# Clustered attention and two mixers on one core: the place of the scores in an attention step, of the first u tiles and of the second batch's u

## The chip, the cores and the metric

The kernel runs on one core of one Trainium2 chip. Its time is the device time of one execution in microseconds (us). The kernel before takes 904.54 us (median of 3 runs, 904.22 to 904.85). A core has five engines, each with an instruction queue of its own that it works through in order: TensorE (PE in the profile; its weight loads, PEld, overlap its matmuls), VectorE (DVE), ScalarE (ACT), GpSimd (POOL) and SyncE (SP), which here only issues transfers (DMA).

## The reference

Attention in which a query sees only the keys of its own cluster, then two mixer layers. All inputs are 32-bit or 64-bit floats on the host.

```python
# attention: batch 2, heads 8, sequence 768, head size 64, 16 clusters
q_assign = argmax(q_n . c_n); k_assign = argmax(k_n . c_n)
scores = where(q_assign == k_assign, q @ k.T / 8, -1e9)
x = softmax(scores) @ v                     # as [2, 768, 512]
# first mixer: U [768, 32], V [32, 768], 4*512 hidden channels
u = x + ((x.T @ U) @ V).T
x = u + relu(u @ w_ch1) @ w_ch2
# second mixer: 256 hidden tokens, 1536 hidden channels
u = x + (relu(x.T @ w_tok1) @ w_tok2).T
out = u + relu(u @ w_ch1) @ w_ch2
```

## The kernel before

**Precision.** Operands of the large products are split into two parts, hi and lo (`rnd` rounds to the hi part, mostly on ACT; `sub` makes the lo part, mostly on DVE), and a product is the sum of hi x hi, hi x lo and lo x hi. The mixers' weights come as 64-bit floats and are turned into 32-bit ones on the chip by `conv` (one operation on ACT, four on DVE for each block of 512 columns) and then split. One call of `tick` moves this conversion on by one block through its stages.

**Attention** works in head pairs: 2 batches x 4 pairs, 12 tiles of 128 queries each, 96 tiles. For tile n, `s_mm` makes the scores (four matmuls of 384 columns into banks 0 and 1 or 2 and 3 of PSUM, by turns), `s_max` takes the negated row maximum on DVE (`nm`), `s_exp` the exponential on ACT with its row sum (`p32`, three buffers), `t_mm` transposes the six blocks of 128 columns on PE into banks 4 and 5, four blocks to a bank, `t_out` makes the hi part (`pth`, ACT) and the lo part (`ptl`, DVE) of each finished bank, and `pv` multiplies with v. A group of three tiles is transposed while the group before is multiplied with v; `pv_out` and `merge` bring its result back to rows, and `merge_out` scales it into `xn`.

The order is written by hand in `step(n)`: the exponential of tile n+1, the transposes that fill a bank and their hi and lo parts, the scores and maximum of tile n+2, the other transposes, then work of other parts at set steps (`mid`, then PV, then `late`). A step with n even finishes one bank, one with n odd two. At set steps of a pair stand the cluster assignment of the next pair (`scores`, `argmax_a`, `argmax_b`), its copies into the stacks `qk` by some 22 transfers on SP, the load and split of v, the product of `xn` with U (`zmm`), and for the first batch the addition of (x.T U) V (`zadd`). Seven conversion ticks stand in the last 20 steps.

**The first mixer** works in three passes over 512 of the 1536 tokens (batch and sequence in one row of tokens), with 16 blocks of 128 hidden channels each. `half_slots` gives turns: `hidden(k+1)` with its relu and split (`hidden_out`: `gh` on ACT, `gl` on DVE), then `outmm(k)`, 12 matmuls of 512 columns each. In the first pass each half slot also takes one tick, so the weights are converted just ahead of their use; the split ones go through DRAM for the two later passes. `umm` transposes a tile of `xn` on PE and `umm_out` makes its hi and lo parts `uh` and `ul`, the mixer's input. Four tiles of u (0 to 3) are made between attention and the first hidden layer; the others, and the second batch's `zadd`, in `rest_of_u`, one operation in each half slot from the start of the first pass. Near the end of a pass `outmm` adds uh and ul into `x2` (`f == nf - 3`) and then the result to it; `x2` lies over `xn` with its rows in another order, c by batch and token, so that its first tokens lie over tiles of both batches.

**The second mixer** first mixes tokens (`tok(0)`, `tok(1)`), beside the third pass of the first mixer and the first pass of its own channel part, then has three passes of 12 blocks.

## Time and profile before

| what | value |
|---|---|
| time, median of 3 runs | 904.54 us |
| the profiled execution | 905.5 us |
| its span | 903.7 us |
| PE busy | 801.8 us (89%) |
| weight loads (PEld) busy | 654.9 us (72%) |
| DVE busy | 535.1 us (59%) |
| ACT busy | 352.9 us (39%) |
| POOL busy | 101.4 us (11%) |
| mean granted TensorE clock | 0.976 of full |

The profile is of one execution. Busy time is the sum of an engine's instructions; matmuls overlap, so a PE that is always busy is not yet PE at its peak. Attention takes the span up to about 360 us, the two mixers the rest. A timeline row gives the start, the length, the engine, the line of the kernel, and the operation with its output and inputs by their names in the kernel; in square brackets stands how long the engine had been idle before it, and what it waited for. An instruction's length reaches past the start of the next one on its engine, so what an operation costs its engine is read from start to start.

### The profile page before, as it was taken

What the parts mean: (1) busy time and instruction counts of PE and PEld (TensorE: products, weight loads), DVE (VectorE), ACT (ScalarE), POOL (GpSimd) and SP (SyncE); (2) the same over time, 40 slices, a digit from 0 to 9 for tenths busy, and PEclk for the clock granted to TensorE, in tenths of its full rate; (3) what the DMA queues carried; (4) which work ended last, traced back from release to release, by engine and by line L of the source; (5) the groups of instructions that cost most, each with busy time, mean ns of one, the idle gap of its engine ahead of it and who ended that gap; (6) DMA issues with size and microseconds to landing.
All of it is one profiled execution on the core that took longest, in us unless ns stands there. A gap on an engine that the chain in (4) does not pass through costs nothing.

```text
span 903.7 us, 11114 instructions
## 1 busy us (share of the span) xinstructions
PE 801.8 (89%) x3989; PEld 654.9 (72%) x3989; DVE 535.1 (59%) x857; ACT 352.9 (39%) x679; POOL 101.4 (11%) x88
## 2 busy tenths in 40 slices
PE   1787878888888877989988999999999999999998
PEld 0566666777666665866656888888888888888886
DVE  3778667676768577699889778766233123212213
ACT  1675656656656665344343323343122111111110
POOL 1110110110101001000002222322120011000000
PEclk9998999899999999899999999999999999999999
DMA  8725152433425313377888899997545444654762
GB/s 203 158 61 132 46 139 53 115 79 88 90 77 113 113 48 106 126 267 271 282 299 290 326 377 370 404 399 301 201 137 175 140 140 140 250 191 164 268 196 94
DMA packets 59238, 167.78 MB, mean 186 GB/s; under 512 B 8656, under 2 KB 16848, under 8 KB 59184
## 3 DMA queue, kind: packets, MB, share of 16 engines
q1 hardware_dynamic: 57984, 164.95, 55.5%
q10 hardware_dynamic: 1200, 2.13, 1.0%
q8 instruction: 31, 0.51, 0.2%
q14 instruction: 23, 0.19, 0.1%
HBM read 114.10 MB, written 32.51 MB: 162 GB/s over the span
## 4 chain that ended last, share of the span: by engine, by line
PE 49%; DVE 28%; ACT 11%; SPq 4%; issue 4%; DMA 3%; ACTq 0%; DVEq 0%
PE ps L73 47%; DVE nm L261 7%; DVE ptl L85 5%; ACT p L266 5%; ACT pth L78 3%; DVE c L104 3%; DVE c L105 2%; DVE qk L85 2%; DMA vraw<-in_v_dram 2%; DVE c L103 2%; ACT qk L78 2%; SPq L238 1%; DVE c L100 1%; SPq L237 1%; DVE am L198 1%
## 5 line engine op out<-in xcount | busy, mean ns | idle before, releaser
L73 PE MATMUL ps<-uh,qk 128*128 128x512 f32 x672 | 224.3, 395 | 6.0 <-ACT qk L78 5.4
L73 PE MATMUL ps<-gh,qk 128*128 128x512 f32 x672 | 222.5, 392 | 0.2
L606 DVE SCALAR_TENSOR_TENSOR gl<-ps,gh 128x512 fp32r<-128x512 f32 x84 | 57.8, 689 | 194.7 <-ACT gh L605 194.7
L275 PE MATMUL ps<-ident,p 128*128 128x128 f32 x576 | 105.3, 294 | 58.8 <-DVE ptl L85 46.0
L73 PEld LDWEIGHTS ps<-uh,qk 128*128 128x128 f32 x672 | 126.0, 188 | 37.1 <-ACT qk L78 7.9
L85 DVE TENSOR_TENSOR ptl<-ps,pth 128x512 fp32r<-128x512 f32 x144 | 98.6, 685 | 88.0 <-ACT pth L78 86.8
L73 PEld LDWEIGHTS ps<-gh,qk 128*128 128x128 f32 x672 | 126.6, 188 | 26.7 <-issue 1.0
L275 PEld LDWEIGHTS ps<-ident,p 128*128 128x128 f32 x576 | 70.2, 147 | 97.6 <-DVE ptl L85 82.2
L605 ACT ACTIVATE gh<-ps 128x512 fp32r<-128x512 f32 x84 | 49.9, 594 | 226.1 <-PE ps L73 225.9
L73 PE MATMUL ps<-gl,qk 128*128 128x512 f32 x336 | 132.2, 393 | 3.9 <-DVE gl L606 3.7
L73 PE MATMUL ps<-ul,qk 128*128 128x512 f32 x336 | 131.3, 391 | 0.3 <-DVE ul L85 0.3
L266 ACT ACTIVATE p<-ps,nm 128x768 f32<-128x768 f32 x96 | 86.3, 899 | 109.0 <-DVE nm L261 108.8
L261 DVE TENSOR_REDUCE nm<-ps 128x1 f32<-128x768 f32 x96 | 90.9, 947 | 8.6 <-PE ps L73 8.6
L78 ACT ACTIVATE pth<-ps 128x512 fp32r<-128x512 f32 x144 | 81.0, 592 | 1.0 <-PE ps L275 0.7
L73 PEld LDWEIGHTS ps<-gl,qk 128*128 128x128 f32 x336 | 63.3, 188 | 19.6 <-DVE gl L606 6.9
L73 PE MATMUL ps<-pth,vhl 128*128 128x384 f32 x192 | 76.4, 398 | 0.6 <-ACT osb L291 0.6
L73 PEld LDWEIGHTS ps<-ul,qk 128*128 128x128 f32 x336 | 63.3, 188 | 13.1 <-DVE ul L85 0.6
L73 PE MATMUL ps<-ptl,vhl 128*128 128x384 f32 x192 | 68.3, 356 | 1.6 <-DVE ptl L85 1.6
L73 PE MATMUL ps<-qk 112*128 112x384 f32 x192 | 50.5, 389 | 11.3 <-DMA qk<-om 11.3
L73 PE MATMUL ps<-qk,qk 112*128 112x384 f32 x192 | 47.8, 372 | 0.0
L105 DVE SCALAR_TENSOR_TENSOR c<-c,c 128x512 int32<-128x512 int32 (+1 forms) x63 | 46.0, 729 | 2.2
L104 DVE SCALAR_TENSOR_TENSOR c<-c,c 128x512 int32<-128x512 int32 (+1 forms) x63 | 45.0, 714 | 2.2
(121 smaller groups left out, 862.1 us busy)
## 6 DMA issues: line engine op xcount, KB each, us to landing
qk<-scr_b SPq DMA_DIRECT2D x72, 512.0 KB, 3.3
qk<-scr_a SPq DMA_DIRECT2D x64, 512.0 KB, 8.0
c<-in_wa_dram SPq DMA_DIRECT2D x32, 512.0 KB, 4.2
scr_a<-qk SPq DMA_DIRECT2D x32, 512.0 KB, 4.1
c<-in_wb_dram SPq DMA_DIRECT2D x24, 512.0 KB, 7.4
scr_b<-chl SPq DMA_DIRECT2D x24, 512.0 KB, 7.4
qk<-sq__89 SPq DMA_DIRECT2D x15, 384.0 KB, 4.0
qk<-sk__90 SPq DMA_DIRECT2D x29, 192.0 KB, 3.0
```

Source lines behind the costliest of these rows:

```text
L73: pe.matmul(o, lhsT=l, rhs=r, start=start, stop=stop, **kw)
L78: act.activation(o, i, AF.Copy, scale=scale)
L85: eng.tensor_tensor(out=o, in0=a, in1=b, op=ALU.subtract)
L100: dve.tensor_scalar(out=dst, in0=dst, scalar1=2.0 ** -15, scalar2=122879.9921875, op0=ALU.max, op1=ALU.min)
L103: dve.tensor_scalar(out=d, in0=d, scalar1=3, scalar2=0x3FFFFFF8, op0=ALU.logical_shift_left, op1=ALU.bitwise_and)
L104: dve.scalar_tensor_tensor(out=d, in0=lo, scalar=29, in1=d, op0=ALU.logical_shift_right, op1=ALU.bitwise_or)
L105: dve.scalar_tensor_tensor(out=d, in0=hi, scalar=-0x40000000, in1=d, op0=ALU.bitwise_and, op1=ALU.bitwise_or)
L261: dve.tensor_reduce(out=nm[:, n % 4 : n % 4 + 1], in_=ps[:, b0 : b0 + 2, 0:HS], axis=AX.XY, op=ALU.max, negate=True)
L266: act.activation(p32[n % NP32].rearrange("p (j k) -> p j k", j=2), ps[:, b0 : b0 + 2, 0:HS], AF.Exp, bias=nm[:, n % 4 : n % 4 + 1], accum_ ...
L275: pe.transpose(ps[:, TB + j % 2, ts(i, P)], p32[n % NP32][:, ts(c, P)], ident)
L605: act.activation(gh, o, AF.Relu)
L606: dve.scalar_tensor_tensor(out=gl, in0=o, scalar=0.0, in1=f32(gh), op0=ALU.max, op1=ALU.subtract)
```

## The change

In `step` the scores and the maximum of tile n+2 move to the head, ahead of the exponential of tile n+1. The first four tiles of u are made in the last two attention steps, into banks 0 to 3 which no scores use any more. For that u is held by pass: pass 0's (`u0`) lies in the buffer of the odd head pairs (`qk1`, now allocated for the whole kernel, with the conversion's `chl` in its upper part), the others where u was. The first hidden layer follows the last PV product, ahead of the last merge. `x2` is now held by batch over `xn` of the same batch, so an addition that crosses batches or passes is cut in two (`pieces`). `rest_of_u` now takes one operation in three half slots, with ten between the eighth and the ninth, and so reaches into the second pass with the second batch's last four u tiles.

```diff
@@ -115,11 +115,13 @@
     xn = fp.tile([P, NB, NPAIR, NS, P], F32, name="xn")
     NW = 3
-    qk0 = fp.tile([P, 8 * S], F32R, name="qk0")
+    qk0, qk1 = (fp.tile([P, 8 * S], F32R, name=f"qk{i}") for i in range(2))
     whl = [qk0[:, ts(i, 2048)].rearrange("p (i h n) -> p i h n", i=2, h=2) for i in range(NW)]
     c64 = [fp.tile([P, 512], I64, name=f"c64_{i}") for i in range(4)]
     c32 = [fp.tile([P, 512], F32, name=f"c32_{i}") for i in range(3)]
-    chl = [fp.tile([P, 2, 512], F32R, name=f"chl_{i}") for i in range(2)]
+    u0 = [qk1[:, ts(i, 2048)].rearrange("p (c n) -> p c n", c=NC) for i in range(2)]
+    chl = [qk1[:, ts(4 + i, 1024)].rearrange("p (h n) -> p h n", h=2) for i in range(2)]
     ap_ctx = ExitStack()
     ap = ap_ctx.enter_context(tc.tile_pool(name="ap", bufs=1))
@@ -127,8 +129,7 @@
     KA, KB0, NST = 112, 96, 2
-    set0 = [qk0[:, ts(i, 2 * S)].rearrange("p (h s) -> p h s", h=2) for i in range(4)]
-    set1 = [ap.tile([P, 2, S], F32R, name=f"qk1{i}") for i in range(4)]
+    set0, set1 = ([x[:, ts(i, 2 * S)].rearrange("p (h s) -> p h s", h=2) for i in range(4)] for x in (qk0, qk1))
     qS, kS = [set0[0:2], set1[0:2]], [set0[2:4], set1[2:4]]
     sq_ = ap.tile([P, 2, S], F32, name="sq_")
@@ -332,8 +333,8 @@
             pe.transpose(ps[:, bk, ts(c, P)], xn[:, b, c, t, :], ident)
     def umm_out(b, t, bk):
-        k = b * S + t * P
-        uh, ul = (x[:, :, k : k + P] for x in fst["u"])
+        p, k = divmod(b * S + t * P, TW)
+        uh, ul = (x[:, :, k : k + P] for x in fst["u"][p])
         o = ps[:, bk, :].rearrange("p (c k) -> p c k", c=NC)
         rnd(act, uh, o)
         sub(dve, ul, o, f32(uh))
@@ -545,19 +546,22 @@
         for k in range(3):
             at(late, s + k, uv[i][k])
     at(late, 13, vst_split)
+    for t in range(TW // P):
+        at(mid, NTILE - 2 + t // 2, lambda t=t: umm(0, t, t))
+        at(late, NTILE - 2 + t // 2, lambda t=t: umm_out(0, t, t))
     NTICK = 7
     for i in range(NTICK):
         at(late, NTILE - 20 + 3 * i, tick)
     def step(n):
+        if n + 2 < NTILE:
+            s_mm(n + 2)
+            s_max(n + 2)
         if n + 1 < NTILE:
             s_exp(n + 1)
         j, i = divmod(NS * n, 4)
         t_mm(n, 0, 4 - i)
         t_out(j)
-        if n + 2 < NTILE:
-            s_mm(n + 2)
-            s_max(n + 2)
         t_mm(n, 4 - i, NS)
         if i:
             t_out(j + 1)
@@ -594,7 +598,7 @@
         wh, wl = (whl[k % NW][:, 0, j, :] for j in range(2))
         o = ps[:, bk, :]
         for c in range(NC):
-            u_h, u_l = (t[:, c, ts(p, TW)] for t in fst["u"])
+            u_h, u_l = (t[:, c, :] for t in fst["u"][p])
             mm(o, wh[:, ts(c, P)], u_h, c == 0, False)
             mm(o, wh[:, ts(c, P)], u_l, False, False)
             mm(o, wl[:, ts(c, P)], u_h, False, c == NC - 1)
@@ -616,26 +620,31 @@
             mm(o, wh[:, cs], gh, f == 0, False)
             mm(o, wh[:, cs], gl, False, False)
             mm(o, wl[:, cs], gh, False, f == nf - 1)
-        uh, ul = fst["u"]
-        tok_ = ts(p, TW)
+        uh, ul = fst["u"][p]
         if f == nf - 3:
-            for c in range(NC):
-                dve.tensor_tensor(out=x2[:, c, tok_], in0=f32(uh[:, c, tok_]), in1=f32(ul[:, c, tok_]), op=ALU.add)
+            for b, s, n, k in pieces(p * TW, TW):
+                for c in range(NC):
+                    dve.tensor_tensor(out=x2[b][:, c, s : s + n], in0=f32(uh[:, c, k : k + n]), in1=f32(ul[:, c, k : k + n]), op=ALU.add)
         if f == nf - 1:
             for c in range(NC):
-                o = x2[:, c, tok_]
-                dve.tensor_tensor(out=o, in0=ps[:, c, :], in1=o, op=ALU.add)
-                if m:
-                    s0 = p * TW
-                    while s0 < p * TW + TW:
-                        b, s = divmod(s0, S)
-                        n = min(S - s, p * TW + TW - s0)
-                        sp.dma_start(out[b, c][:, s : s + n], x2[:, c, s0 : s0 + n])
-                        s0 += n
-    x2 = xn.rearrange("p b a t c -> p (b a t c)").rearrange("p (c s) -> p c s", c=NC)
+                for b, s, n, k in pieces(p * TW, TW):
+                    o = x2[b][:, c, s : s + n]
+                    dve.tensor_tensor(out=o, in0=ps[:, c, k : k + n], in1=o, op=ALU.add)
+                    if m:
+                        sp.dma_start(out[b, c][:, s : s + n], o)
+    def pieces(s0, n, size=S):
+        i, k = s0, 0
+        while k < n:
+            b, s = divmod(i, size)
+            w = min(size - s, n - k)
+            yield b, s, w, k
+            i, k = i + w, k + w
+    x2 = [xn[:, b].rearrange("p c t k -> p c (t k)") for b in range(NB)]
+    fst["u"] = [u0, None, None]
     setup()
     s_exp(0)
@@ -645,13 +654,14 @@
     for c in range(NS):
         pv(last, c)
     pv_out(last)
+    hidden(0)
     merge(G - 1, 1)
     merge_out(G - 1, 1)
     ap_ctx.close()
     tp = ctx.enter_context(tc.tile_pool(name="tp", bufs=1))
-    fst["u"] = [tp.tile([P, NC, NB * S], F32R, name=f"u{n}") for n in "hl"]
     fst["g"] = [[tp.tile([P, TW], F32R, name=f"g{n}{i}") for i in range(2)] for n in "hl"]
+    fst["u"][1:] = [[tp.tile([P, NC, TW], F32R, name=f"u{p}{n}") for n in "hl"] for p in range(1, NPASS)]
     xnh = tp.tile([P, NS, CD], F32R, name="xnh")
     xnl = tp.tile([P, NS, CD], F32R, name="xnl")
     yh = tp.tile([P, NDT, CD], F32R, name="yh")
@@ -659,11 +669,6 @@
     t1h, t1l = fst["t1"] = [tp.tile([P, NS, DT], F32R, name=f"t1{n}") for n in "hl"]
     t2h, t2l = fst["t2"] = [tp.tile([P, NDT, S], F32R, name=f"t2{n}") for n in "hl"]
     t32 = [tp.tile([P, HS], F32, name=f"t32_{i}") for i in range(2)]
-    for t, bk in enumerate((5, 0, 1, 2)):
-        umm(0, t, bk)
-        umm_out(0, t, bk)
-    hidden(0)
     def half_slots():
@@ -683,7 +688,6 @@
     def tok(b):
         bk = [6]
-        uh, ul = fst["u"]
         def nbk():
             bk[0] = 13 - bk[0]
@@ -692,7 +696,7 @@
         for s in range(NS):
             k = nbk()
             for c in range(NC):
-                pe.transpose(ps[:, k, ts(c, P)], x2[:, c, b * S + s * P : b * S + s * P + P], ident)
+                pe.transpose(ps[:, k, ts(c, P)], x2[b][:, c, ts(s, P)], ident)
             act.copy(xnh[:, s, :], ps[:, k, :])
             sub(dve, xnl[:, s, :], ps[:, k, :], f32(xnh[:, s, :]))
             yield
@@ -719,11 +723,12 @@
                     mm(o, yl[:, t, ts(c, P)], t2h[:, t, hs_], False, False)
                     mm(o, yh[:, t, ts(c, P)], t2l[:, t, hs_], False, t == NDT - 1)
                 t_ = t32[c % 2]
-                cols = slice(b * S + h * HS, b * S + h * HS + HS)
-                dve.tensor_tensor(out=t_, in0=o, in1=x2[:, c, cols], op=ALU.add)
-                rnd(act, uh[:, c, cols], t_)
-                sub(pool, ul[:, c, cols], t_, f32(uh[:, c, cols]))
+                dve.tensor_tensor(out=t_, in0=o, in1=x2[b][:, c, hs_], op=ALU.add)
+                for p, s, n, i in pieces(b * S + h * HS, HS, TW):
+                    uh, ul = (x[:, c, s : s + n] for x in fst["u"][p])
+                    rnd(act, uh, t_[:, i : i + n])
+                    sub(pool, ul, t_[:, i : i + n], f32(uh))
                 yield
     done = 0
@@ -744,9 +749,11 @@
         ops = [(lambda bk: zmm(G - 1, bk), lambda bk: zmm_out(G - 1))]
-        u_ = [(umm, umm_out, 0, t) for t in range(TW // P, NS)] + [(umm, umm_out, 1, t) for t in range(NS)]
-        z_ = [(zadd, zadd_out, 1, t) for t in range(NS)]
-        order = [x for p in zip(u_, z_) for x in p] + u_[NS:]
+        u_, z_ = ([(f, o, b, t) for b in range(NB) for t in range(NS)] for f, o in ((umm, umm_out), (zadd, zadd_out)))
+        order = u_[4:6] + z_[6:8] + u_[6:8]
+        for i in range(8, 12):
+            order += z_[i : i + 1] + u_[i - 1 : i] * (i > 8)
+        order.append(u_[11])
         for f, o, b, t in order:
             ops.append((lambda bk, f=f, b=b, t=t: f(b, t, bk), lambda bk, o=o, b=b, t=t: o(b, t, bk)))
         for i in range(len(ops) + 1):
@@ -754,7 +761,8 @@
                 ops[i - 1][1](6 + (i - 1) % 2)
             if i < len(ops):
                 ops[i][0](6 + i % 2)
-            yield
+            for _ in range(3 if i != 7 else 10):
+                yield
     end = lambda m, p: 2 * (NFA * (p + 1) if m == 0 else NFA * NPASS + NFB * (p + 1)) + 1
```

On DVE, in the last steps of a head pair before the cluster assignment, there stood (`nm` is the maximum of tile n+2, `ptl` a lo part of tile n; `am` is the assignment):

```order
L85 TENSOR_TENSOR ptl<-ps,pth 128x512
L261 TENSOR_REDUCE nm<-ps 128x1
L85 TENSOR_TENSOR ptl<-ps,pth 128x512
L261 TENSOR_REDUCE nm<-ps 128x1
L85 TENSOR_TENSOR ptl<-ps,pth 128x512
L192 STREAM_TRANSPOSE am_91<-ps 128x384
L197 TENSOR_REDUCE amx<-am_91 128x24
L198 TENSOR_TENSOR am_92<-am_91,amx 128x384
L199 TENSOR_TENSOR am_92<-am_92,wcl 128x384
L85 TENSOR_TENSOR ptl<-ps,pth 128x512
L261 TENSOR_REDUCE nm<-ps 128x1
```

and now stands:

```order
L262 TENSOR_REDUCE nm<-ps 128x1
L85 TENSOR_TENSOR ptl<-ps,pth 128x512
L262 TENSOR_REDUCE nm<-ps 128x1
L85 TENSOR_TENSOR ptl<-ps,pth 128x512 x2
L193 STREAM_TRANSPOSE am_86<-ps 128x384
L198 TENSOR_REDUCE amx<-am_86 128x24
L199 TENSOR_TENSOR am_87<-am_86,amx 128x384
L200 TENSOR_TENSOR am_87<-am_87,wcl 128x384
L262 TENSOR_REDUCE nm<-ps 128x1
L85 TENSOR_TENSOR ptl<-ps,pth 128x512
```

The maximum has moved ahead of the lo parts of its step, and the two lo parts of an odd step now stand together.

On PE, in a step with an even tile and the next one, there stood (`ps<-ident,p` are transposes, `qk` scores, `pth` and `ptl` PV products):

```order
L275 MATMUL ps<-ident,p_0_100 128x128 x4
L73 MATMUL ps<-qk_72 128x384 x4
L275 MATMUL ps<-ident,p_0_100 128x128 x2
L73 MATMUL ps<-pth,vhl_98 128x384
L73 MATMUL ps<-ptl,vhl_98 128x384
L73 MATMUL ps<-pth,vhl_98 128x384
L73 MATMUL ps<-ptl,vhl_98 128x384
L275 MATMUL ps<-ident,p_1_101 128x128 x2
L73 MATMUL ps<-qk_72 128x384 x4
L275 MATMUL ps<-ident,p_1_101 128x128 x4
```

and now stands:

```order
L73 MATMUL ps<-qk_72 128x384 x4
L276 MATMUL ps<-ident,p_0_95 128x128 x6
L73 MATMUL ps<-pth,vhl_93 128x384
L73 MATMUL ps<-ptl,vhl_93 128x384
L73 MATMUL ps<-pth,vhl_93 128x384
L73 MATMUL ps<-ptl,vhl_93 128x384
L73 MATMUL ps<-qk_72 128x384 x4
L276 MATMUL ps<-ident,p_1_96 128x128 x6
```

The scores have moved ahead of all six transposes of the step.

On PE, from the last merge to the first mixer's U product, there stood (`ps<-ii,osb` is the merge, `ps<-ident,xn` the u tiles, `uh` and `ul` the first hidden layer, `xn,u_sb` the U product):

```order
L73 MATMUL ps<-ii,osb_106 128x64
L332 MATMUL ps<-ident,xn 128x128 x16
L73 MATMUL ps<-uh,qk_72 128x512
L73 MATMUL ps<-ul,qk_72 128x512
L73 MATMUL ps<-uh,qk_72 128x512 x2
L73 MATMUL ps<-ul,qk_72 128x512
L73 MATMUL ps<-uh,qk_72 128x512 x2
L73 MATMUL ps<-ul,qk_72 128x512
L73 MATMUL ps<-uh,qk_72 128x512 x2
L73 MATMUL ps<-ul,qk_72 128x512
L73 MATMUL ps<-uh,qk_72 128x512
L73 MATMUL ps<-xn,u_sb 32x128 x6
```

and now stands, with the hidden layer's inputs named `qk` and two groups of eight u transposes further up, one in each of the last two steps:

```order
L73 MATMUL ps<-pth,vhl_94 128x384
L73 MATMUL ps<-ptl,vhl_94 128x384
L73 MATMUL ps<-qk_73,qk_72 128x512 x12
L73 MATMUL ps<-ii,osb_100 128x64
L73 MATMUL ps<-ii,osb_101 128x64
L73 MATMUL ps<-ii,osb_100 128x64
L73 MATMUL ps<-ii,osb_101 128x64
L73 MATMUL ps<-ii,osb_100 128x64
L73 MATMUL ps<-ii,osb_101 128x64
L73 MATMUL ps<-xn,u_sb 32x128 x6
L73 MATMUL ps<-qk_73,qk_72 128x512 x12
L73 MATMUL ps<-gh_2683,qk_72 128x512
```

The hidden layer now follows the PV products, the merge stands behind it, and the sixteen transposes are gone from between them.

## Rows read from the trace of the kernel before

**Rows 1.** Windows: busy us (xcount) of PE, PEld, DVE, ACT, POOL; clock, DMA share, GB/s

```profile
26.00:360.50 334.50, 271.59 (x1645) 225.61 (x1646) 241.45 (x379) 205.57 (x421) 36.74 (x32) 0.96 0.37 94
...
520.00:540.00 20.00, 20.00 (x90) 16.57 (x89) 13.64 (x20) 6.41 (x12) 4.76 (x4) 1.00 0.98 376
```

**Rows 2.** Timeline, one round in attention: start us, length us, engine, line, operation

```profile
225.00 0.95 DVE L261 TENSOR_REDUCE nm<-ps 128x1 f32<-128x768 f32 x1
...
226.04 0.90 ACT L266 ACTIVATE p<-ps,nm 128x768 f32<-128x768 f32 x1 [0.95 <-DVE nm L261]
...
226.93 1.07 ACT L78 ACTIVATE pth<-ps 128x512 fp32r<-128x512 f32 x2
...
227.56 0.69 DVE L85 TENSOR_TENSOR ptl<-ps,pth 128x512 fp32r<-128x512 f32 x1 [1.61 <-ACT pth L78]
...
228.16 0.95 DVE L261 TENSOR_REDUCE nm<-ps 128x1 f32<-128x768 f32 x1
```

**Rows 3.** Timeline, the same exponential of two head pairs, six pairs apart

```profile
73.53 0.90 ACT L266 ACTIVATE p<-ps,nm 128x768 f32<-128x768 f32 x1 [5.35 <-DVE nm L261]
...
321.51 0.90 ACT L266 ACTIVATE p<-ps,nm 128x768 f32<-128x768 f32 x1 [1.68 <-DVE nm L261]
```

**Rows 4.** Timeline of DVE in the first pass of the first mixer

```profile
425.42 0.69 DVE L105 SCALAR_TENSOR_TENSOR c<-c,c 128x512 int32<-128x512 int32 x1
...
427.23 0.68 DVE L85 TENSOR_TENSOR qk<-c,qk 128x512 fp32r<-128x512 f32 x1
...
433.11 0.69 DVE L105 SCALAR_TENSOR_TENSOR c<-c,c 128x512 int32<-128x512 int32 x1
...
434.50 0.69 DVE L85 TENSOR_TENSOR qk<-c,qk 128x512 fp32r<-128x512 f32 x1
...
436.75 0.69 DVE L105 SCALAR_TENSOR_TENSOR c<-c,c 128x512 int32<-128x512 int32 x1
...
438.13 0.69 DVE L85 TENSOR_TENSOR qk<-c,qk 128x512 fp32r<-128x512 f32 x1 [0.69 <-ACT qk L78]
```

**Rows 5.** Timeline of PE, from one tile's transposes to the next tile's

```profile
124.17 0.60 PE L275 MATMUL ps<-ident,p 128*128 128x128 f32 x4
...
126.24 0.38 PE L275 MATMUL ps<-ident,p 128*128 128x128 f32 x2
```

**Rows 6.** Timeline, work that some steps of a head pair add

```profile
195.42 0.57 DVE L192 STREAM_TRANSPOSE am<-ps 128x384 f32<-128x384 f32 x1
...
197.91 0.68 DVE L85 TENSOR_TENSOR ptl<-ps,pth 128x512 fp32r<-128x512 f32 x1
...
199.37 0.54 DVE L204 TENSOR_REDUCE amx<-am 128x24 f32<-128x384 bf16 x1
...
201.11 0.65 DVE L85 TENSOR_TENSOR ptl<-ps,pth 128x512 fp32r<-128x512 f32 x1
...
203.15 0.94 DVE L218 SCALAR_TENSOR_TENSOR sq__89<-sq__89 128x768 fp32r<-128x768 f32 x1
...
205.62 1.45 PE L73 MATMUL ps<-ii,osb 128*128 128x64 f32 x12
...
209.46 0.16 DVE L301 TENSOR_SCALAR rr<-rs 128x6 f32<-128x6 f32 x1
...
210.55 0.69 DVE L85 TENSOR_TENSOR ptl<-ps,pth 128x512 fp32r<-128x512 f32 x1
...
212.28 0.58 SPq L174 DMA_DIRECT2D vraw<-in_v_dram  x1
...
215.73 0.94 ACT L78 ACTIVATE vhl<-vraw 128x384 fp32r<-128x384 f32 x2 [0.35 <-DMA vraw<-in_v_dram]
```

**Rows 7.** Timeline of PE, between attention and the first mixer

```profile
363.35 0.52 PE L73 MATMUL ps<-ptl,vhl 128*128 128x384 f32 x1
...
374.19 1.50 PE L73 MATMUL ps<-xn,u_sb 128*32 128x128 f32 x12
```

**Rows 8.** Timeline of PE, four transposes behind a wait

```profile
72.62 1.11 PE L275 MATMUL ps<-ident,p 128*128 128x128 f32 x4 [3.46 <-DVE ptl L85]
```

## The prediction

> **What bounds the kernel now.** I read the split of the span by windows first. Attention runs from the first exponential at 26.0 us to the last lo block at about 360.5 us, 334.5 us for 96 tiles, or 3.48 us a tile, and no engine fills it: PE is busy 271.6 us, DVE 241.5, ACT 205.6, at a granted clock of 0.96 [rows 1]. A stage in which no engine is full and time passes at a fixed beat is held by a chain. The timeline shows it: a maximum starts on DVE at 225.00, its exponential on ACT at 226.04, the rounding of a transposed block at 226.93, its lo part on DVE at 227.56, and the next maximum at 228.16 [rows 2]. That is 1.04 + 0.89 + 0.63 + 0.60 = 3.16 us round, four links on two engines. The loop exists only because DVE works in order and the maximum of tile n+2 is written behind the lo part of tile n, which waits for ACT, which stands behind the exponential of tile n+1. The six pairs from the second to the seventh take (321.51 - 73.53) / 6 = 41.3 us each [rows 3]: 12 x 3.16 = 37.9, and 3.4 us of other stops.
>
> Of the other stages I read two windows. The second pass of the first mixer is full on PE, 20.00 of 20.00 us at clock 1.00 [rows 1]. The first pass before it is not: there DVE sets the beat of a half slot, 433.11 to 436.75 = 3.64 us [rows 4], against 12 matmuls x 20.00/90 = 2.67 us on PE.
>
> **The change, part by part.** *Scores and maxima at the head.* DVE now takes the maximum of tile n+2 before the lo parts of tile n, so the four links are no longer one loop. What is left for a tile pair is: exponential done, four score matmuls, maximum, exponential. From start to start that is about 1.0 (the exponential with its accumulator) + 1.0 (four matmuls of 384 columns) + 1.04 = 3.1 us, but the scores have two sets of banks, so it is 3.1 us for two tiles. It no longer binds; what is next is each engine's own work per tile, and the order in which they hand over. The maximum now waits for the score matmuls with the lo parts of its tile queued behind it, and by their banks the later transposes; but PE reaches those scores before the tile's transposes, so the lo parts could not start sooner.
>
> PE: with work at hand it goes from the transposes at 124.17 to the next at 126.24 = 2.07 us a tile [rows 5]; I take 2.1. DVE: a maximum 0.95 and 1.5 lo parts at 0.61 on average, so 1.56 us in a tile with one finished block and 2.17 in one with two. To these come the extras of a pair, each at its step (r0 to r11): on DVE the first half of the argmax 195.42 to 197.91 = 2.49 at r11, the second 199.37 to 201.11 = 1.74 at r0, the lo part of q 0.94 at r1, a merge with its reciprocal 209.46 to 210.55 = 1.09 at r3 and r9; on PE the merge 1.3 at r3 and r9 [rows 6], the U product 1.4 at r5 (1.50 long [rows 7]) and the assignment scores at r10, about 0.8 as four matmuls. I let each step cost the larger of the two engines, as if they could not run ahead of one another: r0 3.3, r1 3.1, r2 2.1, r3 3.4, r4 2.1, r5 3.5, r6 to r8 6.3, r9 3.4, r10 2.9, r11 4.7, together 34.8, and 0.4 for the residual adds that fall into some pairs: 35.2 us. Against 41.3 that is 6.1 us a pair, 36.6 us for six.
>
> Two things pull from that value in both directions. If the engines could slip freely, a pair would cost PE's own sum, 12 x 2.07 + 2.6 + 1.4 + 0.8 = 29.6, with the residual adds 30 us. Against it stand the half clock after a stall, where the same four transposes take 1.11 instead of 0.60 us behind a wait of 3.46 [rows 5, 8], and SP's chain (a rival below). I take these as cancelling. The first pair has DVE work of its own (converting U and V, the argmax of the second pair) and a PE still at the low clock: I give it 3 us. The last has four conversion ticks on DVE, each 434.50 + 0.60 to 436.75 + 0.61 = 2.26 us [rows 4], that fill the DVE idle time which the loop left, and the work of the next part: 1 us. Attention: 36.6 + 3 + 1 = 40.6 us less. The bounds are nothing (the loop re-forms) and 6 x 11.3 + 4 = 72.
>
> The rule that matmul busy time is a poor measure of how full PE is stands in the Trainium skill (Perfetto Trace Analysis, Identifying the Most-Contended Engine). Read by the busy row, attention could not go under 271.6 us, a gain of at most 63; by the weight loads, which the skill recommends, under 225.6, a gain of up to 109. Neither decides here, since the spacing of 2.07 us a tile is measured.
>
> *First u in the last two tiles.* Before, the last PV matmul ends at 363.35 + 0.52 = 363.87 and the U product starts at 374.19 [rows 7]: 10.3 us for a copy, a merge, 16 transposes, the wait for their hi and lo parts, and the first hidden layer. Now 12 hidden matmuls (2.7 us) and the merge (1.3) stand between, and the wait for the merge's scaling (1.1): 5.1, so 5 us less. The 16 transposes (about 1.7 us) and four lo parts (0.61 each) go into tiles 94 and 95, where the maxima (0.95 each) are already gone; that is why the last pair is given only 1 us. No DMA moves with them.
>
> *Second batch's u in the second pass.* In the first pass an op of this list costs by the half slot that it falls in. In the slot behind a gl the gap from the last conversion op to the next hi-lo part is 1.81 us with it (425.42 to 427.23) and 1.39 without (433.11 to 434.50): 0.42. In the other parity DVE would idle 0.69 for ACT anyway (438.13), which an op of 0.61 fills: nothing [rows 4]. Before, seven ops stand in the costly parity, now three of the six that are left: 4 x 0.42 = 1.7 us less. Three residual products and four tiles of transposes land in the second pass, where PE has no idle time: 3 x 0.22 + 4 x 0.4 = 2.3 us more. The DVE work there is covered, with 13.64 of 20 us busy [rows 1]; uncovered it would be 7 x 0.61 = 4.3.
>
> *Residual by batch.* The middle pass now crosses batches in eight adds of 256 columns instead of four of 512, twice in each mixer, and half of the token mixer's roundings are split in two. I cost it at nothing: DVE, ACT and POOL have 6 to 15 of 20 us free [rows 1], and the next output matmul comes only after a hidden layer of 2.7 us. Uncovered, the eight adds at no more than 0.69 each (the 512-column price) would be 2.8 us a time.
>
> **The sum.** The profiled execution took 905.5 us, 1.8 beyond its span and 1.0 above the median of 904.54. 905.5 - 40.6 - 5.1 - 1.7 + 2.3 = 860.4, and as a median 1.0 less: 859.
>
> **The rivals.** *Free slip.* PE becomes the bound, a pair costs some 31 us, and the first and last give 6: 6 x 10.3 + 6 = 68 less in attention, 832. For it: the banks of scores, blocks and probabilities are double or triple. Against: DVE must do 4.7 + 3.3 + 3.1 = 11.1 us in r11 to r1 while PE has 6.3, and PE waits for its lo parts.
>
> *SP's queue takes over.* ACT splits v at r5, and v's load is issued behind all copies into the stacks. The lo part of q is done at 203.15 + 0.94 = 204.09, and v is split at 215.73, with ACT held 0.35 for it [rows 6]: 11.6 us in which SP issues 13 copies and, at 212.28, the load, one after another, whatever the tiles' pace. My r2 to r5 are 11.1 us. So it is nearly tied already; with slower landings it is 2 us a pair: 12 more, 871. The Trainium skill (Perfetto Trace Analysis, What "DMA-bound" means) calls a stretch bound by its issues where the issuing engine's track is solid with them; by that rule r2 to r5 stay at 11.6 us, and the trace agrees in so far as ACT is the one that waits.
>
> *The loop re-forms.* If the maximum at the head waited for an exponential that waits for the lo parts, say by a bank, the 3.1 us above would be for one tile and not for two. Attention would stay where it was, and 904.5 - 4.5 = 900. Against: each exponential frees its banks a whole tile before they are written again.
>
> *Slower, by the clock.* PE would go to 1.2 GHz through attention. Its pair is then 12 x 2.07 x 2 + 2 x 4.8 = 59 us, so that from a share of about 0.4 of the time at that level a pair costs more than 41.3; at 0.6 it costs 29.6 x 1.6 = 47.4, 6.1 x 8 = 49 more, 950. For it: after waits the half clock is there [rows 8]. Against: 0.96 is granted now, with PE waiting in every tile [rows 1], and the change makes the waits shorter.
>
> **Chances.** My forecast 0.60, with 846 to 872 as its own range; free slip 0.12; SP's queue 0.18; the loop re-formed 0.05; the slow clock and whatever else ends above 904.5, 0.05. The range 838 to 880 leaves out most of the last two and half of the free slip. About 0.2%, 1.8 us, is what a measurement can tell from no change: faster 0.93, within 0.2% 0.02, slower 0.05.
>
> **What would show it.** Right: exponentials spaced 2.1 to 3.5 us instead of 3.16, with the widest at the argmax; the wait of exponentials for maxima much shorter; attention from its first exponential to its last lo block near 294 us; the U product about 5 us behind the last PV matmul; half slots of the first pass at 3.64 us as before. Wrong: exponentials still 3.1 apart, ACT idle several us for v in every pair, a granted clock under 0.9 in attention, or PE waiting in the second pass for gl.

## The result, and the profile after

The changed kernel takes 871.83 us (median of 4 runs, 870.79 to 874.27) against 904.69 for the kernel before in the same session: a ratio of 0.9641, with a 95% interval of 0.9621 to 0.9662. The forecast was 859, with 846 to 872 as the likeliest case's own range. The sign and the broken loop came out; 13 us of the gain did not, and the time lies at the very end of that range, within 1 us of the 871 of the rival *SP's queue takes over*. The profiled execution of after took 874.27 us, 2.0 beyond its span and 2.4 above its median.

Both traces can be laid side by side at a few marks. Between them the spans differ by 31.4 us:

| stretch | before, us | after, us | difference | predicted |
|---|---|---|---|---|
| start to the end of the last PV matmul | 363.87 | 335.12 | -28.75 | -40.6 |
| from there to the last U product | 10.32 | 3.98 | -6.34 | -5.1 |
| from there to the residual adds of the first pass | 119.83 | 119.58 | -0.25 | -1.7 |
| second pass of the first mixer, adds to adds | 86.51 | 89.60 | +3.09 | +2.3 |
| the rest | 323.17 | 324.02 | +0.85 | 0 |

So one line carries the error: attention. The windows of after, in the columns of [rows 1], show the new stretch of attention and a piece of the second pass:

```profile
26.00:333.50 307.50, 267.26 (x1662) 242.32 (x1663) 250.37 (x380) 207.57 (x424) 36.65 (x32) 0.93 0.40 102
...
500.00:520.00 20.00, 20.00 (x92) 16.58 (x91) 15.31 (x21) 7.63 (x14) 5.95 (x4) 1.00 0.97 357
```

Attention lasts 307.5 us instead of 334.5. PE now fills 87% of it and DVE 81%, and the granted clock is 0.93 where it was 0.96 [rows 1]. The second pass stays full on PE, and DVE's 15.31 us are still covered.

The same two exponentials as in [rows 3], with what ACT waited for in brackets:

```profile
68.42 0.90 ACT L267 ACTIVATE p<-ps,nm 128x768 f32<-128x768 f32 x1 [4.76 <-DVE nm L262]
...
291.53 0.90 ACT L267 ACTIVATE p<-ps,nm 128x768 f32<-128x768 f32 x1
```

Six pairs take (291.53 - 68.42) / 6 = 37.18 us each, not 41.33 as before and not the predicted 35.2. The 2.0 us a pair are 11.9 us over six pairs, and the whole attention line misses by 40.6 - 28.75 = 11.85.

That the loop of [rows 2] is gone is seen in the timeline of DVE, here in a stretch without extra work: maxima (L262) and lo parts (L85) no longer wait for one another's round.

```profile
193.18 0.96 DVE L262 TENSOR_REDUCE nm<-ps 128x1 f32<-128x768 f32 x1 [0.20 <-PE ps L73]
194.25 0.69 DVE L85 TENSOR_TENSOR ptl<-ps,pth 128x512 fp32r<-128x512 f32 x1
195.25 0.96 DVE L262 TENSOR_REDUCE nm<-ps 128x1 f32<-128x768 f32 x1 [0.30 <-PE ps L73]
196.12 1.28 DVE L85 TENSOR_TENSOR ptl<-ps,pth 128x512 fp32r<-128x512 f32 x2
```

The maximum here waits 0.2 to 0.3 us for PE, and the lo parts behind it not at all; before, one lo part waited 1.61 [rows 2]. On the pages, the idle time of exponentials for maxima falls from 108.8 to 30.5 us (the line of the exponential, its last entry):

```profile
L266 ACT ACTIVATE p<-ps,nm 128x768 f32<-128x768 f32 x96 | 86.3, 899 | 109.0 <-DVE nm L261 108.8
```

```profile
L267 ACT ACTIVATE p<-ps,nm 128x768 f32<-128x768 f32 x96 | 86.5, 902 | 31.3 <-DVE nm L262 30.5
```

What a pair lost against the plan is in the spacing of its exponentials. In the pair from 175.43 us it is 3.9 3.8 3.2 3.0 1.8 3.2 **6.6** 1.4 2.1 2.9 1.9 3.6; the 6.6, between the exponentials of r5 and r6, is 5.8 to 7.0 in the six pairs. The timeline there, on four engines (SPq is SP's issue of a transfer; L219 the lo part of q, L292 the copy of the PV result, L319 and L320 the casts of the U product, vhl the split of v):

```profile
187.28 0.94 DVE L219 SCALAR_TENSOR_TENSOR sq__84<-sq__84 128x768 fp32r<-128x768 f32 x1
...
188.24 0.51 SPq L234 DMA_DIRECT2D qk<-sq__84  x1
...
194.23 0.90 ACT L267 ACTIVATE p<-ps,nm 128x768 f32<-128x768 f32 x1
...
195.80 1.50 PE L73 MATMUL ps<-xn,u_sb 128*32 128x128 f32 x12
...
196.41 0.58 SPq L175 DMA_DIRECT2D vraw<-in_v_dram  x1
...
198.24 0.48 ACT L292 COPY osb<-ps 128x384 f32<-128x384 f32 x1 [1.69 <-PE ps L73]
198.62 0.25 ACT L319 CAST zst<-ps 32x128 fp32r<-32x128 f32 x1
198.88 0.26 ACT L320 CAST zst<-ps 32x128 fp32r<-32x128 f32 x1
199.98 0.94 ACT L78 ACTIVATE vhl<-vraw 128x384 fp32r<-128x384 f32 x2 [0.84 <-DMA vraw<-in_v_dram]
200.82 0.88 ACT L267 ACTIVATE p<-ps,nm 128x768 f32<-128x768 f32 x1
...
201.85 0.98 PE L73 MATMUL ps<-qk 112*128 112x384 f32 x4 [1.58 <-ACT p L267]
```

ACT works in order and stops twice in a row here: 1.69 us for PE, whose U product stands ahead of the PV matmuls that the copy needs, and 0.84 us for v's load. The exponential behind them leaves late, and PE waits 1.58 us for it. From the end of q's lo part (187.28 + 0.94 = 188.22) to the split of v it is 11.76 us, with 13 copies and the load on SP between, where [rows 6] gave 11.6.

The transition, answering [rows 7]: last PV matmul, the first hidden layer, the merge, the U product.

```profile
334.78 0.34 PE L73 MATMUL ps<-ptl,vhl 128*128 128x384 f32 x1
334.95 2.93 PE L73 MATMUL ps<-qk,qk 128*128 128x512 f32 x12
337.72 1.45 PE L73 MATMUL ps<-ii,osb 128*128 128x64 f32 x12
339.10 1.56 PE L73 MATMUL ps<-xn,u_sb 128*32 128x128 f32 x12
```

PE has no gap left in it: 335.12 to 339.10 is 3.98 us, not the predicted 5.1, since the U product did not wait the 1.1 us for the merge's scaling: DVE scales at 339.20, when the U product has begun with the tiles of the first half, which an earlier merge had scaled.

### The profile page after: what moved, and what is told of

It is laid out like the page before. It is cut to its first block, busy times and chain, and to the rows that moved or that the text cites. A ratio compares the mean times of both kernels' runs of the same rounds, so it can differ in the third digit from the quotient of the medians.

```text
span 872.3 us, 11264 instructions
## 1 busy us (share of the span) xinstructions
PE 793.5 (91%) x3989; PEld 666.1 (76%) x3989; DVE 542.7 (62%) x873; ACT 353.4 (41%) x687; POOL 102.1 (12%) x96
## 4 chain that ended last, share of the span: by engine, by line
PE 62%; DVE 23%; DMA 5%; ACT 4%; SPq 4%; issue 2%; DVEq 0%; ACTq 0%
PE ps L73 58%; PE ps L276 4%; DVE ptl L85 3%; DVE nm L262 3%; DVE c L104 3%; DVE c L105 3%; DVE qk L85 2%; ACT qk L78 2%; DVE c L100 2%; DVE c L103 2%; DMA qk<-scr_a 2%; DVE am L199 1%; DMA vraw<-in_v_dram 1%; SPq L239 1%; SPq L238 1%
## 5 line engine op out<-in xcount | busy, mean ns | idle before, releaser
L276 PE MATMUL ps<-ident,p 128*128 128x128 f32 x576 | 90.6, 290 | 27.0 <-DVE ptl L85 26.7
L73 PE MATMUL ps<-qk 112*128 112x384 f32 (+1 forms) x384 | 93.0, 368 | 23.4 <-ACT p L267 11.4
L262 DVE TENSOR_REDUCE nm<-ps 128x1 f32<-128x768 f32 x96 | 91.3, 951 | 28.4 <-PE ps L73 28.0
L85 DVE TENSOR_TENSOR ptl<-ps,pth 128x512 fp32r<-128x512 f32 x144 | 94.9, 685 | 21.5 <-ACT pth L78 18.3
L267 ACT ACTIVATE p<-ps,nm 128x768 f32<-128x768 f32 x96 | 86.5, 902 | 31.3 <-DVE nm L262 30.5
L73 PEld LDWEIGHTS ps<-qk 112*128 112x128 f32 (+1 forms) x384 | 74.8, 208 | 31.2 <-ACT p L267 18.2
L73 PE MATMUL ps<-qk,qk 128*128 128x512 f32 x336 | 86.2, 400 | 10.2 <-ACT qk L78 10.2
L73 PEld LDWEIGHTS ps<-qk,qk 128*128 128x128 f32 x336 | 61.0, 188 | 31.0 <-ACT qk L78 14.6
L73 PE MATMUL ps<-u2h,qk 128*128 128x512 f32 x224 | 74.1, 392 | 0.0
L73 PE MATMUL ps<-u1h,qk 128*128 128x512 f32 x224 | 73.9, 391 | 0.0
L78 ACT ACTIVATE qk<-c 128x512 fp32r<-128x512 f32 x56 | 35.3, 631 | 93.5 <-DVE c L105 60.6
L85 POOL TENSOR_TENSOR qk<-c,qk 128x512 fp32r<-128x512 f32 x28 | 39.5, 1410 | 150.9 <-ACT qk L78 150.9
```

Of the source, the lines that this page charges most:

```text
L73: pe.matmul(o, lhsT=l, rhs=r, start=start, stop=stop, **kw)
L78: act.activation(o, i, AF.Copy, scale=scale)
L85: eng.tensor_tensor(out=o, in0=a, in1=b, op=ALU.subtract)
L262: dve.tensor_reduce(out=nm[:, n % 4 : n % 4 + 1], in_=ps[:, b0 : b0 + 2, 0:HS], axis=AX.XY, op=ALU.max, negate=True)
L267: act.activation(p32[n % NP32].rearrange("p (j k) -> p j k", j=2), ps[:, b0 : b0 + 2, 0:HS], AF.Exp, bias=nm[:, n % 4 : n % 4 + 1], accum_ ...
L276: pe.transpose(ps[:, TB + j % 2, ts(i, P)], p32[n % NP32][:, ts(c, P)], ident)
```

## The experiments

Ratios are to the kernel before in the same session (its median was 904.7 to 906.0). "Spacing" is the time of one pair over six pairs, from the same two exponentials as above, in each kernel's own trace.

| kernel | median, us | ratio, 95% interval | spacing, us |
|---|---|---|---|
| before | 904.7 | 1 | 41.33 |
| changed kernel | 871.8 | 0.9641, 0.9621 to 0.9662 | 37.18 |
| order_alone | 875.2 | 0.9667, 0.9635 to 0.9699 | 36.99 |
| rest_alone | 900.9 | 0.9953, 0.9935 to 0.9971 | 41.40 |
| u_first | 872.0 | 0.9631, 0.9610 to 0.9652 | 37.08 |
| early_v | 865.5 | 0.9559, 0.9533 to 0.9586 | 35.88 |
| zmm_late | 870.5 | 0.9627, 0.9588 to 0.9666 | 36.96 |
| v_and_zmm | 856.9 | 0.9464, 0.9442 to 0.9486 | 34.61 |
| klo_r1 | 872.0 | 0.9632, 0.9616 to 0.9648 | 36.87 |
| v_zmm_klo | 854.6 | 0.9431, 0.9411 to 0.9450 | 34.70 |
| k_at_r0 | 852.2 | 0.9409, 0.9388 to 0.9431 | 33.71 |
| q_lo_r2 | 845.9 | 0.9349, 0.9337 to 0.9360 | 33.12 |

**order_alone** and **rest_alone** split the change in two. The first makes the change's edit of `step` alone in the kernel before; the second undoes that edit in the changed kernel:

```diff
     def step(n):
-        if n + 2 < NTILE:
-            s_mm(n + 2)
-            s_max(n + 2)
         if n + 1 < NTILE:
             s_exp(n + 1)
         j, i = divmod(NS * n, 4)
         t_mm(n, 0, 4 - i)
         t_out(j)
+        if n + 2 < NTILE:
+            s_mm(n + 2)
+            s_max(n + 2)
         t_mm(n, 4 - i, NS)
```

> The kernel before with one edit: scores and maxima of tile n+2 stand at the head of the step. No first u in the last tiles, no residual by batch, the list of the rest of u as before. Theory (the parts add up): the trace of the changed kernel has attention 27 us shorter (six pairs 19.1, first 4.9, last 2.9), and all of it comes from this edit: 904.7 - 27 = 877.7, range 875 to 880, wait of exponentials for maxima about 24 us instead of 84 between 60 and 300 us. Rival A (what fell on the first and last pair, 2.9 to 7.8 us, belongs to the other edits): 881 to 885. Rival B (the freed banks and the other residual layout have a share of the shorter pairs too): over 885.

> The changed kernel with the step's order put back: scores and maxima of tile n+2 between the two runs of transposes. Theory (the parts add up): transition and first pass give 8.6 us, the second pass takes 3.1 back, attention stays as before: 904.7 - 8.6 + 3.1 = 899.2, range 897 to 901; the six middle pairs stay near 41.3 us. Rival (the parts lean on one another: the roundings of the first u cost the last two tiles more while the loop still binds): over 901.

Measured: 875.2 and 900.9, 3.3% and 0.5% less than before, together 3.8% where the whole change gives 3.6%; within the intervals the parts add up. The spacing of a pair moves with the order alone (36.99, against 41.40 without it). Rivals A and B fall. The time of rest_alone lies too near the rival's bound of 901 to part it from the theory; its trace does: from the last exponential to the end of the last PV matmul it takes 9.46 us with the first u there, and 10.10 before without it, so the last tiles did not pay for it while the loop stood.

**u_first** prices the list of the rest of u:

```diff
-            for _ in range(3 if i != 7 else 10):
-                yield
+            yield
```

> The changed kernel with the list of the rest of u worked at one op in each half slot, as before, so that all of it lies in the first pass (the changed kernel takes one in three, with a gap of ten after the eighth). Theory (the prediction's terms: 4 ops x 0.42 us in the first pass against 7 in the second): the second pass of the first mixer gives 3.1 back, the first takes 1.7 to 2: 870 to 871.5. Rival (ops in the first pass are covered by PE's idle time): 868 to 869.5. Rival (an op in the first pass costs more than 0.42, since DVE sets the beat there): 873 to 876.

Measured: 872.0, the intervals lie over one another. In its trace the second pass takes 548.75 - 461.83 = 86.92 us instead of 89.60, and the way from the U product to the first adds 461.83 - 340.85 = 120.98 instead of 119.58; the other 1.3 us lie elsewhere and below what the medians can tell. Putting u into the second pass neither gains nor loses more than about 2 us, the width of the intervals.

**early_v** and **zmm_late** take one of the two stops at r5 each:

```diff
             at(late, s1 - 6, lambda g=n: load_pair(g))
+            at(late, s1 - 5, lambda g=n: load_v(g))
...
-            if n > 1:
-                at(late, s1 + 3, lambda g=n: load_v(g))
```

```diff
-            at(mid, s0 + NTT + 5, lambda g=g: zmm(g, MB))
-            at(late, s0 + NTT + 5, lambda g=g: zmm_out(g))
+            at(late, s0 + NTT + 5, lambda g=g: zmm(g, MB))
+            at(late, s0 + NTT + 6, lambda g=g: zmm_out(g))
```

> The changed kernel with the load of v of the next pair issued at r7 of the pair before its old place at r3, ahead of all copies into the stacks; nothing else. Theory SP (the load of v at the end of SP's queue holds ACT at r5): ACT's wait for it (5.0 us over five pairs) is gone and so is that time: 871.8 - 5 = 867, range 865 to 869. Theory ACT (the exponential at r5 stands behind the copy of the PV result and two casts of the U product, which wait for PE): ACT waits elsewhere, part of the 5 us comes back as other waits: 868 to 872. Theory PE clock and argmax: no change, 871 to 872.

> The changed kernel with the U product of a pair behind the PV matmuls of r5 (it stood ahead of them), and its two casts on ACT and one lo part on DVE a step later, at r6; nothing else. Theory ACT: at r5 ACT waits 1.7 us for PE at the copy of the PV result and then casts before it may split v and start the exponential; 1.0 to 1.7 us a pair come back over seven pairs: 7 to 12 us, 860 to 865, and the interval of exponentials at r5 to r6 falls from 5.8-7.0 to about 5 us. Theory SP: ACT then waits for v's load instead, which lands at the same distance from the lo part of q: 870 to 872, with ACT's waits for v grown by the same amount. Theory PE clock and argmax: 870 to 872 with that interval unchanged.

Measured: 865.5 for the early load, as theory SP expected; 870.5 for the late U product, as theory SP expected too. The waits of ACT between 60 and 300 us (total, times, longest) tell why the second edit came to nothing. In the changed kernel:

```profile
ACT osb L292 <- PE ps L73: 15.1, 19, 1.7
ACT vhl L78 <- DMA vraw<-in_v_dram: 5.0, 5, 1.2
```

With the late U product:

```profile
ACT vhl L78 <- DMA vraw<-in_v_dram: 17.7, 6, 3.6
ACT osb L292 <- PE ps L73: 4.4, 12, 0.5
```

10.7 us of waiting for PE went and 12.7 us of waiting for v came. Its timeline at r5 shows the stop in one piece:

```profile
194.44 0.48 ACT L292 COPY osb<-ps 128x384 f32<-128x384 f32 x1
197.92 0.94 ACT L78 ACTIVATE vhl<-vraw 128x384 fp32r<-128x384 f32 x2 [3.00 <-DMA vraw<-in_v_dram]
198.76 0.88 ACT L267 ACTIVATE p<-ps,nm 128x768 f32<-128x768 f32 x1
```

The copy no longer waits; v does, 3.00 us, and the exponential comes as late as before: the interval at r5 is 5.5 to 7.3 us in the six pairs.

**v_and_zmm** makes both edits.

> Both single edits in the changed kernel: v's load at r7 of the pair before, and the U product behind the PV matmuls of r5 with its casts at r6. Alone the first gave 865.5 and the second 870.5 (its casts no longer stood ahead, but ACT's wait for v grew from 5.0 to 17.7 us). Theory (two stops at r5 in a row, each of which hides the other): together more than the sum of 6.3 and 1.4; the interval r5 to r6, 5.8 with the early load, falls to about 4, 1.8 us in each of seven pairs less: 865.5 - 12 = 853, range 850 to 858. Rival (only v's load mattered): 864 to 866. Rival (the sum): 861 to 864.

Measured: 856.9. Against the changed kernel the two edits give 0.8% and 0.1% alone and 1.8% together: two stops in a row, each hiding the other. The spacing says the same: 1.30 and 0.22 us a pair alone, 2.57 together. The interval at r5 falls from 6.6 to 3.6 us, that of r6, where the two casts now stand, grows from 1.4 to 2.6, and the timeline of ACT has no wait left at r5:

```profile
187.34 0.48 ACT L292 COPY osb<-ps 128x384 f32<-128x384 f32 x1
187.72 0.94 ACT L78 ACTIVATE vhl<-vraw 128x384 fp32r<-128x384 f32 x2
188.55 0.89 ACT L267 ACTIVATE p<-ps,nm 128x768 f32<-128x768 f32 x1
```

Its spacing, 34.61 us, is within 0.6 of the predicted 35.2. That is in part luck: r9 takes 1.8 where 3.4 was priced and r4 3.2 where 2.1 was, and two more edits below bring the spacing to 33.1.

**klo_r1** and **v_zmm_klo** move POOL's lo part of k (the latter with the two edits above):

```diff
-            at(late, s1, lambda: k_lo(pool, Rk))
...
             at(late, s1 + 1, lambda: mask_rows(pool))
+            at(late, s1 + 1, lambda: k_lo(pool, Rk))
```

> The changed kernel with the lo part of k on POOL one step later, behind the mask rows at r1, so that it no longer runs beside the first comparison of the argmax (1.65 us beside it, 0.56 in the setup without). Theory (POOL's long op draws that comparison out, and DVE holds the pair at r11 to r2): the comparison takes 0.56, the intervals 3.9 and 3.8 together lose about 1 us; 4 to 6 us over six pairs, 866 to 868. Rival 1 (POOL then draws out a later op of DVE by as much): 871 to 873. Rival 2 (SP's copies wait for this lo part, so v's load lands later): slower, 873 to 878.

> All three edits together: early load of v, U product and its casts late at r5 and r6, lo part of k at r1. With v's load out of SP's queue the later lo part of k costs nothing there. If POOL's draw on the comparison counts, 4 to 6 us under the kernel with the first two edits; if POOL draws out another op of DVE instead, equal to it within 2 us.

Measured: 872.0 and 854.6: alone nothing, and with the other edits 2.3 us, whose interval touches that of v_and_zmm, while the spacing does not fall (34.70 against 34.61): no gain is shown. The groups of DVE between 60 and 300 us (busy us, then mean ns of one) show that the theory held for the comparison (L199) and rival 1 for the next operation (L219, the lo part of q). In the changed kernel:

```profile
L199 DVE TENSOR_TENSOR am<-am,amx 128x384 bf16<-128x384 f32 x6 | 9.9, 1646 | 0.2
...
L219 DVE SCALAR_TENSOR_TENSOR sq__84<-sq__84 128x768 fp32r<-128x768 f32 x6 | 5.6, 938 | 0.0
```

With POOL's operation at r1:

```profile
L219 DVE SCALAR_TENSOR_TENSOR sq__84<-sq__84 128x768 fp32r<-128x768 f32 x6 | 8.4, 1404 | 0.0
...
L199 DVE TENSOR_TENSOR am<-am,amx 128x384 bf16<-128x384 f32 x6 | 3.3, 558 | 0.2
```

One lost 1.09 us a time, the other gained 0.47. Alone, r0 falls from 3.8 to 2.7 us, but r2 rises by 0.5, and r5 stays at 5.8 to 7.4, with 6.0 us of waiting for v in all.

**q_lo_r2** and **k_at_r0** look for a place where POOL's operation draws nothing out. The first adds to v_zmm_klo one edit, the second to v_and_zmm another:

```diff
-            at(late, s1 + 1, lambda: q_lo(dve, Rq))
+            at(late, s1 + 2, lambda: q_lo(dve, Rq))
```

```diff
-            at(late, s1 - 1, k_hi)
...
+            at(late, s1, k_hi)
             at(late, s1, lambda: k_lo(pool, Rk))
```

> The kernel with three edits (v's load early, U product and casts late, lo part of k on POOL at r1), and the lo part of q on DVE one step later, at r2. There POOL's long op of 1.82 us no longer runs beside the lo part of q, which took 1.41 beside it and 0.94 before. Theory (only those DVE ops whose two inputs both lie in SBUF are drawn out by POOL; beside maxima and lo parts of blocks, which read PSUM, POOL's op costs nothing): both the comparison (0.56) and the lo part of q (0.94) are short, 0.47 us a pair, 1.5 to 4 us less than the 854.6 of the three edits: 851 to 853. Rival (DVE is drawn out by the same sum wherever POOL's op falls): 854 to 856, with maxima over 0.95 or lo parts over 0.69 beside it. Rival (the copies of q's lo part, a step later, now come late for the scores of the next pair): over 856, with a wait of PE for SP's copies at r10.

> The kernel with two edits (v's load early, U product and casts late), and ACT's hi part of k at r0 instead of r11, so that POOL's lo part of k (still issued at r0) starts about one step later, beside a maximum, a block's lo part and the second half of the argmax. Theory (two inputs in SBUF): the first comparison falls from 1.64 to 0.56; of the second half only the comparison with two inputs in SBUF (0.56 before) is drawn out, by what is left of POOL's op, 0 to 1 us, while the reductions, the transpose, the maximum and the lo part keep 0.54, 0.58, 0.95 and 0.68: 0 to 6 us under the 856.9 of the two edits. Rival (any DVE op beside POOL's is drawn out): maximum or lo part there longer by some tenths, time as 856.9.

Measured: 845.9 and 852.2. Both operations are short in the first (timeline of POOL and DVE at r1 and r2):

```profile
169.47 1.81 POOL L85 TENSOR_TENSOR sk__85<-sk__85 128x768 fp32r<-128x768 f32 x1
169.50 1.27 DVE L85 TENSOR_TENSOR ptl<-ps,pth 128x512 fp32r<-128x512 f32 x2
170.70 0.94 DVE L262 TENSOR_REDUCE nm<-ps 128x1 f32<-128x768 f32 x1
...
172.16 0.95 DVE L219 SCALAR_TENSOR_TENSOR sq__84<-sq__84 128x768 fp32r<-128x768 f32 x1
```

Two lo parts of blocks and a maximum run beside POOL's 1.81 us in 1.27 and 0.94, their usual lengths; each has an input in PSUM. In k_at_r0 POOL's operation (169.24 to 171.10) fell between the two comparisons of the argmax (at 168.48 and 171.38), and both took 0.56; beside it stood a maximum (0.95), a lo part (0.68) and a reduction with one input (0.54), all of their usual lengths. The rival that DVE pays the same wherever POOL's operation falls is out. This agrees with the Trainium skill (GPSIMD Engine Reference, Key points), which says that POOL shares its SBUF interfaces with VectorE and collides with DVE instructions that have two inputs in SBUF.

k_at_r0 is the cleaner price of the collision: against v_and_zmm the intervals at r11 and r0 go together from 7.6 to 6.6 us in five of the six pairs, as much as the comparison lost, and the kernel is 0.6% faster, with intervals that do not touch.

q_lo_r2 is the fastest version run: 3.0% under the changed kernel, 7.4 us under v_zmm_klo by ratio where 1.5 to 4 were expected. Its edit does two things at once. Four of its pairs are 0.9 to 1.3 us shorter, of which the shorter lo part of q explains 0.5; besides, this operation no longer stands ahead of the maximum at r2, whose interval falls by 0.7 to 1.3 us, but ahead of the one at r3, where there is room. The second pair went from 39.3 to 37.0 and the seventh from 36.4 to 33.5, mostly at r4 (4.7 to 3.0 and 4.6 to 3.0 us). There PE ran at half its clock in v_zmm_klo, behind a wait for a lo part on DVE:

```profile
248.91 0.66 PE L276 MATMUL ps<-ident,p 128*128 128x128 f32 x4 [1.32 <-DVE ptl L85]
...
251.92 1.48 PE L73 MATMUL ps<-qk 112*128 112x384 f32 x4
```

The granted clock is 0.64 from 76.0 to 80.8 us and 0.63 from 250.2 to 254.8. In q_lo_r2 PE has no such wait there, and the clock is 1.00 (74.0 to 77.5 and 240.2 to 243.5).

## Why the prediction was right and where it failed

**Right: the loop.** That a reordering on DVE breaks a loop of four links is shown by order_alone: it brings 3.3 of the 3.6%, the exponentials of the changed kernel are 1.3 to 7.0 us apart in place of a beat of 3.2, and their wait for maxima fell by 78 us. Of the signs named, two did not come: the widest interval is at r5, not at the argmax, and attention took 307.5 us, not 294.

**Wrong in size: the term of 35.2 us a pair, and with it the 40.6 of attention.** It measured 37.18, and 28.75. The step that failed is the one that weighed SP's chain against free slip and "took these as cancelling". They did not: with both stops at r5 out of the way the engines gave 34.61 a pair (v_and_zmm), 0.6 below the sum by steps, and the stops put 2.6 on top. Step by step the pair from 175.43 us took 3.9 at r11 (predicted 4.7), 3.8 and 3.2 at r0 and r1 (3.3, 3.1), 3.0 at r2 (2.1), 1.8 and 3.2 at r3 and r4 (3.4, 2.1), 6.6 at r5 (3.5), 6.4 at r6 to r8 (6.3), 1.9 and 3.6 at r9 and r10 (3.4, 2.9): only r5 is far out once neighbours are taken together.

The rival *SP's queue takes over* had named the place (the split of v at r5) and the length (11.6 us from q's lo part, 11.76 measured). By the rule of the Trainium skill (Perfetto Trace Analysis, What "DMA-bound" means) the stretch was to stay at 11.6 us, and the trace agrees: SP's issues follow one another from 188.24 to 196.99 us. That its price (2 us a pair, 2.0 measured against 35.2) and its time (871) fit is luck. The price was for slower landings and came from no row, and the landing did not slow: from the load's issue to the split of v it took 3.45 us before and 3.57 after. Moving the load alone gave 1.30 us a pair. What the rival did not have is that ACT stops twice there: the U product ahead of the PV matmuls fills part of the same wait, so the wait that the trace puts down to v's load (5.0 us in all) is less than what its removal gave (7.8 us over the six pairs by the spacing).

The priced step r5, 3.5 us, counted PE and DVE alone; ACT's queue, with copy, two casts and the split in front of an exponential, was in no step. With both stops gone the interval at r5 is 3.6. So the forecast had the change right and the remainder wrong: what was left of a pair after the loop was bound at r5 by two queues, SP's and ACT's, and not by the larger of PE and DVE.

**Also in that term, with opposite signs.** The steps r11 to r1 were summed at 4.7 + 3.3 + 3.1 = 11.1 us and came out as 3.9 + 3.8 + 3.2 = 10.9, but part of it was not work. Beside POOL's lo part of k, DVE's first comparison took 0.98 us in the kernel before, where it takes 0.56 alone; these 0.42 us are inside the 2.49 that I had read as the cost of the argmax, so a collision looked like a fixed price. The change let the comparison start earlier beside POOL's operation, and it took 1.65. Before and after:

```profile
195.35 1.83 POOL L85 TENSOR_TENSOR sk__90<-sk__90 128x768 fp32r<-128x768 f32 x1 [18.04 <-ACT sk__90 L78]
...
196.61 0.98 DVE L198 TENSOR_TENSOR am<-am,amx 128x384 bf16<-128x384 f32 x1
```

```profile
179.47 1.83 POOL L85 TENSOR_TENSOR sk__85<-sk__85 128x768 fp32r<-128x768 f32 x1 [15.16 <-ACT sk__85 L78]
...
180.07 1.65 DVE L199 TENSOR_TENSOR am<-am,amx 128x384 bf16<-128x384 f32 x1
```

In both the comparison ends 0.41 to 0.42 us after POOL's operation (197.59 behind 197.18, 181.72 behind 181.30): starting earlier gained it nothing.

**First and last pair.** From the first exponential to the first marked one 4.97 us went, not 3; from the second marked one to the last PV matmul it took 1.23 more, not 1 less. The two misses cancel. The first u is 1.9 us of the second: from the last exponential to the end of the PV matmuls it is 13.65 us in the changed kernel and 11.71 in order_alone, which has no first u there. Its eight transposes take 1.92 us in one of the two tiles, at a granted clock of 0.50, and 1.04 in the other, at 1.00 (the trace of after at 325.65 and 328.85), so part of this is PE at half its clock.

**The transition.** 6.34 instead of 5.1 (the sum took off the 5.1 us that were to remain; 10.3 - 5.1 is 5.2, hardly other): the wait for the merge's scaling was not there. Little of this stayed saved, as the next paragraph shows.

**First and second pass.** The 1.7 us less of the first pass measured 0.25, the 2.3 more of the second 3.09. The half slot itself was read rightly, as DVE's rows show: with a lo part of u 404.21 to 406.02 = 1.81, without 1.39, and 3.64 for the slot, all as in [rows 4].

```profile
396.93 0.69 DVE L105 SCALAR_TENSOR_TENSOR c<-c,c 128x512 int32<-128x512 int32 x1
...
398.32 0.69 DVE L85 TENSOR_TENSOR qk<-c,qk 128x512 fp32r<-128x512 f32 x1
...
404.21 0.69 DVE L105 SCALAR_TENSOR_TENSOR c<-c,c 128x512 int32<-128x512 int32 x1
...
406.02 0.68 DVE L85 TENSOR_TENSOR qk<-c,qk 128x512 fp32r<-128x512 f32 x1
...
408.26 0.69 DVE L105 SCALAR_TENSOR_TENSOR c<-c,c 128x512 int32<-128x512 int32 x1
...
411.90 0.69 DVE L105 SCALAR_TENSOR_TENSOR c<-c,c 128x512 int32<-128x512 int32 x1
```

The counted slots did pay: of the half slots of the first pass seven took about 4.05 us before (from one conversion operation to the next, as 404.21 to 408.26 here) and three do now, as forecast; most others stay at 3.64 to 3.71 (408.26 to 411.90). What the line lost lies at its start. DVE's conversions set the beat, and the first of the pass's 33 rows of this kind (L105) comes 2.21 us behind the U product now (341.31 and 339.10) where it came 0.22 ahead of it before (373.97 and 374.19), as the U product itself moved forward. So the two lines belong together: 6.34 + 0.25 = 6.59 us, with 6.8 forecast. u_first shows that the choice is worth nothing within what the runs can tell.

**The clock.** I let it be as before; it fell from 0.96 to 0.93 in attention, though PE idled less there (307.50 - 267.26 = 40.2 us, where [rows 1] give 62.9). PE's rows at the argmax of one pair:

```profile
183.63 0.66 PE L276 MATMUL ps<-ident,p 128*128 128x128 f32 x4 [2.10 <-DVE ptl L85]
...
185.26 1.48 PE L73 MATMUL ps<-qk 112*128 112x384 f32 x4
...
188.63 0.87 PE L73 MATMUL ps<-qk 112*128 112x384 f32 x4
```

Behind a wait of 2.10 us four score matmuls take 1.48 us, and later 0.87: the granted clock is 0.59 from 183.7 to 187.0 us (part of it at 1.2 GHz) and 1.00, 2.4 GHz, from 188 to 190. What that is worth depends on the place. At r4 of two pairs of v_zmm_klo, where PE has work at hand, it went with an interval longer by 1.6 us. At the argmax, where DVE holds the pair, no price is seen: klo_r1 has a granted clock of 0.98 from 26 to 270 us against 0.94 in the changed kernel, and the same time. No run changed the clock alone.
